# Filter cross terms moved from the matrix engine to the vector engine, with a new plan of steps, in a fused spectral filter and MLP kernel

## The chip, the cores and the metric

The kernel runs on one core of one Trainium2 chip. The metric is the device time of one execution in microseconds (us), and a number given for a kernel is the median of its runs.

Engines are named as in the profile: PE is the matrix engine (TensorE), PEld its weight loads, DVE is VectorE, ACT is ScalarE, POOL is GpSimd, SP is the engine that issues most DMA transfers (SPq is its queue). "PEclk" is the clock that was granted to PE, as a share of full speed.

## The reference

The first part filters each of eight batches along the sequence with a Fourier transform; the second is an MLP with a "snake" activation.

```python
def _attn_ref(x, filt_r, filt_i):          # x: (8, 3008, 256)
    X = np.fft.rfft(x, axis=1)
    Y = X * (filt_r + 1j * filt_i)[None]   # 1505 frequencies
    return np.fft.irfft(Y, n=3008, axis=1)

def _moe_ref(x, w_in, w_out, alpha):       # x: (24064, 256), d_ff = 2048
    h = x @ w_in
    s = np.sin(alpha * h)
    g = h + s * s / (alpha + 1e-09)
    return g @ w_out
```

## The kernel before

The transform is factored as 3008 = 47 x 64. Each batch passes three spectral stages, with a trip through DRAM (write, then load in another order) between them:

- Stage 1 (8 pieces): a transform of length 47 (`pa` matmuls). The result goes from tile `t` to DRAM buffer `d1` and comes back as tile `t2`.
- Stage 2 (13 pieces, two of 24 classes each): a transform of length 64 (`pb`), an ACT copy to `xf`, multiplication by the filter on DVE, and the inverse transform (`pc`). The result goes from tile `g` through DRAM buffer `d2` to tile `t4`.
- Stage 3 (16 pieces): the inverse of length 47 (`pd`), which fills `y`, the MLP's input.

A complex product needs four real products. The upper 64 partitions of `xf` hold imaginary parts, the lower 64 real parts. The kernel before makes two full 128-partition products on DVE, one with the real and one with the imaginary filter, and lets PE do the crossing: two inverse matmuls per class with two weight tables add up in PSUM.

```python
nc.scalar.copy(out=xf, in_=ps)
pr = []
for k in range(2):
    pt = ppool.tile([128, 2, C], FP16, ...)
    nc.vector.tensor_tensor(out=pt, in0=xf, in1=f_t[k][:, 2 * u:2 * u + 2, :], op=ALU.mult)
    pr.append(pt)
# [...]
for i in range(2):
    for k in range(2):                                   # two matmuls per class
        nc.tensor.matmul(out=ps[:, i, :], lhsT=e_t[:, k, 2 * w + i, :],
                         rhs=pr[k][:, i, :], start=(k == 0), stop=(k == 1))
```

The MLP is a loop of 384 "steps", 48 per batch. A step issues two blocks of the hidden matmul (`ph`), a cosine on ACT, one fused DVE operation that makes the snake (`v`), and about one block of the output projection (`po`, eight matmuls). Spectral pieces of later batches are put in between the steps by a plan: a piece of batch `b` is issued at step 48*b plus the number given.

```python
plan = {1: [-45 + i for i in range(8)],                  # stage 1: -45 to -38
        2: [-29 + 14 * i / 13 for i in range(13)],       # stage 2: from -29
        3: [-10, -9] + [-7 + 2 * i for i in range(14)]}  # stage 3: from -10
# [...]
fps = pool("fps", 2, PSUM)     # the two banks that all spectral matmuls share
hps = pool("hps", 4, PSUM)     # four banks for the hidden matmul
```

## Time and profile before

| | before |
|---|---|
| median (range) of the first three runs | 840.68 us (840.13 to 840.93) |
| PE, DVE, ACT busy | 96%, 75%, 73% |
| inverse matmuls `pc` | 384 |

The first fence has lines of the profile's page of the kernel before: busy time by engine, the busy tenths of PE, DVE and the granted clock in 40 slices of the span, and the shares of the chain of waits.

```profile
PE 799.8 (96%) x5793; PEld 544.2 (65%) x5793; DVE 628.1 (75%) x1119; ACT 613.0 (73%) x1200; POOL 28.3 (3%) x55
PE   5758999999999999999999999999999999999996
DVE  3658886778877788777877788777877778777772
PEclk9969999999999999999999999999999999999999
PE 83%; DMA 7%; ACT 4%; issue 3%; DVE 2%; POOL 0%; SPq 0%; ACTq 0%; DVEq 0%; POOLq 0%
```

PE is full from the fifth slice to the last but one, at full clock, and the chain that ended last is PE work. DVE has a quarter of its time free. The Trainium skill (Trainium Kernel Development and Optimization, "Performance Expectations") warns that matmul busy time is a bad metric for how close a kernel is to roofline, because matmuls are pipelined; here the view by windows helps, since a gap of PE can be seen in it, and it shows none between 150 and 800 us.

Next come two groups of the page before (columns: line, engine, operation, output<-inputs, shapes, count | busy us, mean ns of one | idle before, releaser).

```profile
L187 DVE TENSOR_TENSOR p<-xf,filt 128x512 f16<-128x512 f16 x192 | 72.1, 419 | 4.9 <-ACT xf L183 4.5
L199 PE MATMUL pc<-p,e_t 128*128 128x256 f16 x384 | 59.7, 275 | 2.6 <-DVE p L187 1.5
```

A product lasts 419 ns, but four in a row take 1.43 us, as the timeline of DVE in the kernel before shows (columns: start, length, what, count):

```profile
28.39 1.43 DVE L187 TENSOR_TENSOR p<-xf,filt 128x512 f16<-128x512 f16 x4 [4.54 <-ACT xf L183]
```

So they start (1.43 - 0.42) / 3 = 0.34 us apart: one begins before the other has ended. For `pc`, 275 ns is latency; in the steady part eight matmuls with 256 columns take 0.88 us, 0.110 us each.

### The profile page before, as it was taken

To read this page: it belongs to the slowest core of one execution; us is meant where nothing else is said; L and a number is where in the kernel's file an instruction comes from. 1 tells how busy PE (TensorE), PEld (TensorE's weight loads), DVE (VectorE), ACT (ScalarE), POOL (GpSimd) and SP (SyncE) were. 2 spreads that over 40 slices of the span, in tenths; PEclk is the share of its full clock that TensorE was granted. 3 is DMA by queue.
4 is the path that set the end of the run, shared out by engine and by line. 5 is a ranking of instruction groups with operands and counts; after the bars stand their busy time and mean duration, and the time that the engine had idled before them with its cause. 6 is when DMAs were issued, how large, how long until landed. Compare 5 with 4: busy or idle time off the path is not lost.

```text
span 837.2 us, 16122 instructions
## 1 busy us (share of the span) xinstructions
PE 799.8 (96%) x5793; PEld 544.2 (65%) x5793; DVE 628.1 (75%) x1119; ACT 613.0 (73%) x1200; POOL 28.3 (3%) x55
## 2 busy tenths in 40 slices
PE   5758999999999999999999999999999999999996
PEld 2425676667776677666776677666777677666674
DVE  3658886778877788777877788777877778777772
ACT  4536886787868787787877777777877878677763
POOL 3210000000000000000000000000000000000000
PEclk9969999999999999999999999999999999999999
DMA  9985835185344744266242763447443353421111
GB/s 220 218 255 117 200 89 130 51 174 116 82 135 81 171 99 109 75 141 153 65 130 60 165 137 82 115 91 171 92 96 94 97 113 83 115 58 38 38 40 45
DMA packets 93495, 94.98 MB, mean 113 GB/s; under 512 B 8084, under 2 KB 82852, under 8 KB 93416
## 3 DMA queue, kind: packets, MB, share of 16 engines
q1 hardware_dynamic: 84784, 75.02, 34.5%
q0 software_dynamic: 6704, 18.09, 12.5%
q10 hardware_dynamic: 1928, 0.86, 0.5%
q8 instruction: 45, 0.74, 0.3%
q14 instruction: 34, 0.28, 0.1%
HBM read 58.02 MB, written 49.81 MB: 129 GB/s over the span
## 4 chain that ended last, share of the span: by engine, by line
PE 83%; DMA 7%; ACT 4%; issue 3%; DVE 2%; POOL 0%; SPq 0%; ACTq 0%; DVEq 0%; POOLq 0%
PE po L369 36%; PE ph L354 35%; PE pc L199 4%; PE pa L157 3%; ACT cos L357 2%; PE pd L219 2%; PE pb L180 2%; DMA t<-d 1%; DMA w_out<-in_moe_w_out_dram 1%; DMA d<-g 1%; DMA d_t<-d_tbl 1%; DVE p L187 1%; DMA x<-in_x_dram 1%; DMA filt<-in_filt_i_dram 1%; ACT t L135 1%
## 5 line engine op out<-in xcount | busy, mean ns | idle before, releaser
L358 DVE SCALAR_TENSOR_TENSOR v<-cos,ph 128x512 f16<-128x512 f32 (+1 forms) x768 | 484.0, 672 | 164.0 <-ACT cos L357 163.5
L357 ACT ACTIVATE cos<-ph 128x512 f32<-128x512 f32 (+1 forms) x768 | 411.6, 589 | 153.9 <-PE ph L354 152.5
L369 PE MATMUL po<-w,v 128*128 128x256 f16 x3008 | 400.9, 273 | 2.6 <-DVE w L337 2.6
L354 PE MATMUL ph<-y,w 128*128 128x512 f16 (+1 forms) x1536 | 391.5, 377 | 0.2 <-ACT y L135 0.2
L369 PEld LDWEIGHTS <-v 128*128 128x128 f16 x3008 | 289.0, 98 | 80.9 <-issue 8.7
L354 PEld LDWEIGHTS <-w 128*128 128x128 f16 x1536 | 150.4, 98 | 101.0 <-issue 4.6
L187 DVE TENSOR_TENSOR p<-xf,filt 128x512 f16<-128x512 f16 x192 | 72.1, 419 | 4.9 <-ACT xf L183 4.5
L375 ACT COPY o<-po 128x512 f32<-128x512 f32 x96 | 55.6, 579 | 17.7 <-PE po L369 15.5
L135 ACT CAST t<-pa 96x512 f16<-96x512 f32 x89 | 51.0, 589 | 19.0 <-PE pa L157 18.9
L183 ACT CAST xf<-pb 128x512 f16<-128x512 f32 x96 | 57.0, 595 | 8.1 <-PE pb L180 5.5
L219 PEld LDWEIGHTS <-t 96*128 96x128 f16 x512 | 36.3, 100 | 39.8 <-DMA t<-d 11.8
L199 PE MATMUL pc<-p,e_t 128*128 128x256 f16 x384 | 59.7, 275 | 2.6 <-DVE p L187 1.5
L157 PE MATMUL pa<-x,wf_t 94*96 94x512 f16 x128 | 47.2, 408 | 10.1 <-DMA x<-in_x_dram 6.3
L219 PE MATMUL pd<-wi_t,t 96*128 96x94 f16 x512 | 43.4, 208 | 11.1 <-DMA t<-d 10.9
L135 ACT CAST y<-pd 128x376 f16<-128x376 f32 x82 | 39.1, 479 | 12.5 <-PE pd L219 12.5
L199 PEld LDWEIGHTS <-e_t 128*128 128x128 f16 x384 | 37.6, 99 | 15.6 <-issue 7.1
L180 PE MATMUL pb<-t,d_t 128*128 128x256 f16 x192 | 38.2, 283 | 2.5 <-DMA t<-d 1.5
L135 ACT CAST g<-pc 128x512 f16<-128x512 f32 x64 | 38.7, 605 | 1.6 <-PE pc L199 1.6
L137 DVE CAST t<-pa 96x512 f16<-96x512 f32 x39 | 26.6, 683 | 15.8 <-PE pa L157 15.8
L180 PEld LDWEIGHTS <-d_t 128*128 128x128 f16 x192 | 18.9, 101 | 23.8 <-issue 4.6
L118 POOL DMA_DIRECT2D x<-in_x_dram x32 | 16.7, 524 | 502.8 <-PE pa L157 490.5
L157 PEld LDWEIGHTS <-wf_t 94*96 94x96 f16 x128 | 16.6, 129 | 19.6 <-issue 9.9
(28 smaller groups left out, 94.3 us busy)
## 6 DMA issues: line engine op xcount, KB each, us to landing
d<-t SPq DMA_DIRECT2D x32, 384.0 KB
d<-g SPq DMA_DIRECT2D x64, 192.0 KB
t<-d SPq DMA_DIRECT2D x32, 384.0 KB
x<-in_x_dram POOLq DMA_DIRECT2D x32, 376.0 KB, 6.9
t<-d SPq DMA_DIRECT2D x60, 192.0 KB
out_dram<-o SPq DMA_DIRECT2D x72, 94.0 KB
w_in<-in_moe_w_in_dram POOLq DMA_DIRECT2D x2, 1024.0 KB, 9.2
w_out<-in_moe_w_out_dram POOLq DMA_DIRECT2D x1, 2048.0 KB, 11.6
```

The costliest lines, as they stand in the source:

```text
L135: marks["act"] = nc.scalar.copy(out=dst, in_=src)
L157: marks["pe"] = nc.tensor.matmul(out=ps[0:NK, :], lhsT=wf_t, rhs=st["x"][ch][:, n0:n0 + 2, :], start=True, stop=True)
L180: nc.tensor.matmul(out=ps[:, i, :], lhsT=d_t[:, s, :], rhs=st["t2"][s // 6][:, s % 6, :], start=True, stop=True)
L183: nc.scalar.copy(out=xf, in_=ps)
L187: marks["prod", u] = nc.vector.tensor_tensor(out=pt, in0=xf, in1=f_t[k][:, 2 * u:2 * u + 2, :], op=ALU.mult)
L199: nc.tensor.matmul(out=ps[:, i, :], lhsT=e_t[:, k, 2 * w + i, :], rhs=pr[k][:, i, :], start=(k == 0), stop=(k == 1))
L219: nc.tensor.matmul(out=psv[:, i, :], lhsT=st["t4"][:, 4 * half + i, cb * 128:cb * 128 + 128], rhs=wi_t, start=True, stop=True)
L354: nc.tensor.matmul(out=ps[:, 0:n], lhsT=w1[:, cb, jb * 128:jb * 128 + 128], rhs=y_cols[:, cb, c0:c0 + n], start=(cb == 0), stop=(cb == 1))
L357: nc.scalar.activation(out=cs[:, 0:n], in_=ps[:, 0:n], func=AFT.Sin, bias=float(np.pi / 2))
L358: marks["snake"] = nc.vector.scalar_tensor_tensor(out=v[k][:, jb, 0:n], in0=cs[:, 0:n], scalar=-1.0, in1=ps[:, 0:n], op0=ALU.add, op1=ALU. ...
L369: nc.tensor.matmul(out=pso[k][:, t % 2, :], lhsT=v[k][:, jb, 128 * t:128 * t + 128], rhs=w2[:, jb, :], start=(jb == 0), stop=(jb == 15))
L375: nc.scalar.copy(out=o[:, 0:nb, :], in_=pso[k][:, 0:nb, :])
```

## The change

From batch 2 on (`FUSED = 2`), DVE does the crossing too: two products of 64 partitions that read one half and write the other, one full product, and an addition in place. Then one inverse matmul per class is enough. This takes 6 batches x 24 classes = 144 matmuls from PE and adds two DVE instructions per piece. To make room on DVE, stage 2 is spread over 24 steps instead of 14, fewer PSUM evacuations go to DVE (one in five instead of one in three), and stage 1 and 3 are moved to fit. Stage 3's loads are issued one ahead, and the pool of the products has 6 buffers instead of 4.

```diff
-        flip[0] = (flip[0] + 1) % 3
+        flip[0] = (flip[0] + 1) % 5
@@ (stage 2, cut)
+            if 0 <= u - 1 < 12:
+                new_products(u - 1)
+                prod(nc.vector, 1, u - 1, lo, hi)      # reads partitions 0-63, writes 64-127
+                prod(nc.vector, 1, u - 1, hi, lo)
+                prod(nc.vector, 0, u - 1, every, every)
+            w = u - 1
+            if 0 <= w < 12:
+                p0, p1 = st["p", w]
+                nc.vector.tensor_tensor(out=p0, in0=p0, in1=p1, op=ALU.add)
+                st["p", w].pop()
+            if 0 <= w - 1 < 12:
+                inverse(w - 1)                          # one matmul per class
@@ (stage 3, cut)
+                for c in ([0, 1] if ch == 0 else [ch + 1] if ch < 3 else []):
+                    load_t4(c)
@@ (plan, cut)
-    plan = {1: [-45 + i for i in range(8)],
-            2: [-29 + 14 * i / 13 for i in range(13)],
-            3: [-10, -9] + [-7 + 2 * i for i in range(14)]}
+        if b == 1 and stage < 3:
+            return 8 + i if stage == 1 else 23 + i
+        odd = b % 2
+        return 48 * b - 4 * odd + (-50 + i if stage == 1 else -36 + 24 * i / 13 if stage == 2
+                                   else -6 + i if i < 4 else -1 + 2 * (i - 4))
```

(The signs of two tables change with it: the filter's second copy is negated instead of the inverse table.) In the new plan stage 1 ends at -43 and stage 2 begins at -36: 7 steps where there were 9.

More of the change, by code (lines that the diff above doesn't have):

```diff
@@ L22 @@
 NK = 4 * NS
+FUSED = 2
 def dft_tables():
@@ L92 @@
     xfpool = pool("xf", 3)
-    ppool = pool("pp", 4)
+    ppool = pool("pp", 6)
     gpool = pool("gp", 4)
@@ L171, in stage1, with forward @@
                     st["t2"].append(t2)
+        def forward(u):
+            ps = (ops if b == 0 else fps).tile([128, 2, C], FP32, name=f"pb_{b}_{u}",
+                                               tag="o" if b == 0 else "f")
+            for i in range(2):
+                s = 2 * u + i
+                nc.tensor.matmul(out=ps[:, i, :], lhsT=d_t[:, s, :],
+                                 rhs=st["t2"][s // 6][:, s % 6, :], start=True, stop=True)
+            xf = xfpool.tile([128, 2, C], FP16, name=f"xf_{b}_{u}", tag="xf")
+            nc.scalar.copy(out=xf, in_=ps)
+            st["xf", u] = xf
@@ new lines, in inverse @@
+        def inverse(w):
+            pr = st.pop(("p", w))
+            if w % 3 == 0:
+                st["g"] = gpool.tile([128, 6, C], FP16, name=f"g_{b}_{w}", tag="g")
+            ps = fps.tile([128, 2, C], FP32, name=f"pc_{b}_{w}", tag="f")
+            for i in range(2):
+                for k, pt in enumerate(pr):
+                    nc.tensor.matmul(out=ps[:, i, :], lhsT=e_t[:, k, 2 * w + i, :],
+                                     rhs=pt[:, i, :], start=(k == 0), stop=(k == len(pr) - 1))
+            i0 = 2 * (w % 3)
+            evac(st["g"][:, i0:i0 + 2, :], ps, i0 != 2 if b == 0 else None)
+            if w % 3 == 2:
+                for p in range(2):
+                    a0 = p * NS + 6 * (w // 3)
+                    nc.sync.dma_start(out=d2[a0:a0 + 6, :, :].rearrange("s n c -> n s c"),
+                                      in_=st["g"][64 * p:64 * p + 64, :, :])
@@ new lines, in prod, with new_products, stage2_first @@
+        def prod(eng, k, u, rows, to):
+            marks["prod", u] = eng.tensor_tensor(out=st["p", u][k][to, :, :], in0=st["xf", u][rows, :, :],
+                                                 in1=f_t[k][rows, 2 * u:2 * u + 2, :], op=ALU.mult)
+        def new_products(u):
+            st["p", u] = [ppool.tile([128, 2, C], FP16, name=f"p_{b}_{u}_{k}", tag="p") for k in range(2)]
+        lo, hi, every = slice(0, 64), slice(64, 128), slice(0, 128)
+        def stage2_first(u):
+            if u < 12:
+                forward(u)
+                new_products(u)
+                for k in range(2):
+                    prod(nc.vector, k, u, every, every)
+            if u > 0:
+                inverse(u - 1)
@@ L173, in stage2 @@
         def stage2(u):
             if u < 12:
-                ps = (ops if b == 0 else fps).tile([128, 2, C], FP32, name=f"pb_{b}_{u}",
-                                                   tag="o" if b == 0 else "f")
-                for i in range(2):
-                    s = 2 * u + i
-                    nc.tensor.matmul(out=ps[:, i, :], lhsT=d_t[:, s, :],
-                                     rhs=st["t2"][s // 6][:, s % 6, :], start=True, stop=True)
-                xf = xfpool.tile([128, 2, C], FP16, name=f"xf_{b}_{u}", tag="xf")
@@ L183, in stage2 @@
-                nc.scalar.copy(out=xf, in_=ps)
-                pr = []
-                for k in range(2):
-                    pt = ppool.tile([128, 2, C], FP16, name=f"p_{b}_{u}_{k}", tag="p")
-                    marks["prod", u] = nc.vector.tensor_tensor(out=pt, in0=xf, in1=f_t[k][:, 2 * u:2 * u + 2, :],
-                                                               op=ALU.mult)
-                    pr.append(pt)
-                st["p", u] = pr
-            if u > 0:
-                w = u - 1
-                pr = st.pop(("p", w))
-                if w % 3 == 0:
-                    st["g"] = gpool.tile([128, 6, C], FP16, name=f"g_{b}_{w}", tag="g")
-                ps = fps.tile([128, 2, C], FP32, name=f"pc_{b}_{w}", tag="f")
-                for i in range(2):
-                    for k in range(2):
-                        nc.tensor.matmul(out=ps[:, i, :], lhsT=e_t[:, k, 2 * w + i, :],
-                                         rhs=pr[k][:, i, :], start=(k == 0), stop=(k == 1))
-                i0 = 2 * (w % 3)
-                evac(st["g"][:, i0:i0 + 2, :], ps, i0 != 2 if b == 0 else None)
-                if w % 3 == 2:
-                    for p in range(2):
-                        a0 = p * NS + 6 * (w // 3)
-                        nc.sync.dma_start(out=d2[a0:a0 + 6, :, :].rearrange("s n c -> n s c"),
-                                          in_=st["g"][64 * p:64 * p + 64, :, :])
@@ new lines, in stage2 @@
+                forward(u)
+            if 0 <= u - 1 < 12:
[10 more added lines that the diff above has]
+                inverse(w - 1)
@@ L209, in stage3, with load_t4 @@
+        def load_t4(ch):
+            st["t4", ch] = t4pool.tile([NK, 8, C], FP16, name=f"t4_{b}_{ch}", tag="t4")
+            marks["t4"] = nc.sync.dma_start(out=st["t4", ch], in_=d2_rows[:, 8 * ch:8 * ch + 8, :])
         def stage3(u):
@@ L212, in stage3 @@
             if rest == 0:
-                t4 = t4pool.tile([NK, 8, C], FP16, name=f"t4_{b}_{ch}", tag="t4")
-                marks["t4"] = nc.sync.dma_start(out=t4, in_=d2_rows[:, 8 * ch:8 * ch + 8, :])
-                st["t4"] = t4
+                for c in ([0, 1] if ch == 0 else [ch + 1] if ch < 3 else []):
+                    load_t4(c)
             ps = fps.tile([128, 4, 128], FP32, name=f"pd_{b}_{u}", tag="f")
@@ L219, in stage3 @@
                 nc.tensor.matmul(out=psv[:, i, :],
-                                 lhsT=st["t4"][:, 4 * half + i, cb * 128:cb * 128 + 128],
+                                 lhsT=st["t4", ch][:, 4 * half + i, cb * 128:cb * 128 + 128],
                                  rhs=wi_t, start=True, stop=True)
@@ L226, in spectral @@
             pieces.append((1, lambda u=u: stage1(u)))
-        for u in range(13):
-            pieces.append((2, lambda u=u: stage2(u)))
+        for u in range(13 if b < FUSED else 14):
+            pieces.append((2, lambda u=u: (stage2_first if b < FUSED else stage2)(u)))
         for u in range(16):
@@ L266, in dup_filter @@
         gs = slice(6 * g, 6 * g + 6)
-        for k in range(2):
-            ins = nc.vector.tensor_copy(out=f_t[k][64:128, gs, :], in_=f_t[k][0:64, gs, :])
+        for ins in (nc.vector.tensor_copy(out=f_t[0][64:128, gs, :], in_=f_t[0][0:64, gs, :]),
+                    nc.vector.tensor_scalar(out=f_t[1][64:128, gs, :], in0=f_t[1][0:64, gs, :],
+                                            scalar1=-1.0, scalar2=None, op0=ALU.mult)):
             behind(ins, marks["prod", 3 * g - 2] if g else s1_dve)
@@ L288 @@
         nc.vector.tensor_copy(out=e_t[0:64, 1, gs, :], in_=e_t[64:128, 0, gs, :])
-        nc.vector.tensor_scalar(out=e_t[64:128, 1, gs, :], in0=e_t[0:64, 0, gs, :],
-                                scalar1=-1.0, scalar2=None, op0=ALU.mult)
+        nc.vector.tensor_copy(out=e_t[64:128, 1, gs, :], in_=e_t[0:64, 0, gs, :])
     ones = cpool.tile([128, 128], FP32)
@@ L391, in store, with at_step @@
             p += cnt
-    plan = {1: [-45 + i for i in range(8)],
-            2: [-29 + 14 * i / 13 for i in range(13)],
-            3: [-10, -9] + [-7 + 2 * i for i in range(14)]}
+    def at_step(b, stage, i):
+        if b == 1 and stage < 3:
[3 more added lines that the diff above has]
+                                   else -6 + i if i < 4 else -1 + 2 * (i - 4))
     pending = [(1 + i % 4 + 8 * (i // 4), 0, piece) for i, (_, piece) in enumerate(first[25:])]
@@ L402 @@
         for stage, piece in spectral(b):
-            at_step = 48 * b + plan[stage][at[stage]]
-            if b == 1 and stage < 3:
-                at_step = 8 + at[stage] if stage == 1 else 23 + at[stage]
+            pending.append((at_step(b, stage, at[stage]), b, piece))
             at[stage] += 1
-            pending.append((at_step, b, piece))
     pending.sort(key=lambda p: p[0])
```

## The prediction

> **What bounds the kernel now.** TensorE. The page gives PE 96% busy, DVE 75%, ACT 73%; in the view by windows every 50 us stretch from 150 to 800 us has PE busy for 49.8 to 50.0 us at clock 1.00. The chain of waits is 83% PE. DVE's longest wait is for ACT's cosine (163 us in all), ACT's for the hidden matmul (152 us): followers, not limits. Before the steady part lie about 54 us of start-up, after it about 14 us of tail.
>
> **Removed from PE.** Six batches x 24 classes lose one of two inverse matmuls: 144 matmuls with 256 columns. The page's mean of 275 ns is latency; in the timeline eight such matmuls take 0.88 us, so each is worth 0.110 us. 144 x 0.110 = 15.8 us, all on the bottleneck.
>
> **Added to DVE.** Per piece, four tensor_tensor of 512 elements replace two; half the partitions makes none shorter. In a row the old products start 0.34 us apart although one lasts 0.42 us. The Trainium skill (VectorE: DVE Perf Modes, "Two Vector instructions with no wait between them") says that an instruction whose inputs or output start in another quadrant than the previous one's starts only when all earlier ones are finished. That hits the two crossed products and the one after them. The trace agrees: the crossed filter copies of the start-up do not overlap (two take 1.14 us, mean 0.56). So a piece costs about 0.34 + 3 x 0.42 = 1.6 us instead of 0.68: +66 us over 72 pieces. The evacuation count of 5 instead of 3 moves 43 casts from DVE to ACT (order of instructions): about -24 us DVE, +21 us ACT. DVE rises to roughly 665 us busy, ACT to 635.
>
> **Where it meets the critical path.** I cut the instruction order into MLP steps and summed durations. Before, a stage-2 step has 2.40 us of PE and about 2.1 us of DVE. After, spread over 24 steps, PE has 1.95 to 2.15 us per step and DVE 2.0 to 2.45: DVE becomes the local limit for about half of each batch period, by 0.1 to 0.3 us a step. Four hidden PSUM banks and the piece-long lag of the inverse absorb some 2 us; the rest stalls PE. Estimate: 0.5 to 2 us per batch, 3 to 10 us in all, centre 5.
>
> **Start-up.** The first two loads of stage 3 are now issued together and the w_out load waits for the second; the first projection already waited for w_out. +1 to 2 us. Stage 3 still ends long before its columns are read; it should cost nothing.
>
> **Sum.** 840.7 - 15.8 + 1.5 + 5 = 831.5 us, about 1.1% faster. Range 824.5 to 839. Faster by over 2% (below 823.9) needs no DVE stall and a start-up gain: 0.13. Within 2%: 0.84. Slower by over 2%: 0.03.
>
> **What would show each step.** Inverse matmuls 384 -> 240, PE busy about 15 us less. Four products per piece, the 64-partition ones as long (0.42 us) as the full ones; DVE busy 655 to 690 us. In the windows, stage-2 stretches show DVE above 95% and PE losing 0.5 to 2 us per batch, waiting for DVE (snake freeing hidden banks, or the add before the inverse), while other stretches stay full. First projection 1 to 2 us later.
>
> **What would make it wrong.** Crossed products dearer than 0.45 us: at 0.5 us each the backlog would lose 15 to 25 us, no gain left. Fewer stalls than I assume, or a shorter start-up: down to 822. DVE lag holding an evacuation that PE needs at once makes the slack smaller than 2 us.

## More of the kernel before

Between the last piece of stage 1 and the first of stage 2 lie 9 steps.

Last, the trip through DRAM between stages 1 and 2, for batch 3 (batches count from 0), as the timeline of the kernel before has it:

```profile
275.40 0.60 PE L157 MATMUL pa<-x,wf_t 94*96 94x512 f16 x2
277.24 0.32 SPq L161 DMA_DIRECT2D d<-t  x1
286.03 5.69 SPq L169 DMA_DIRECT2D t<-d  x8
292.32 0.38 PE L180 MATMUL pb<-t,d_t 128*128 128x256 f16 x2
```

The last stage-1 matmul, the issue of the last write, the issue of the loads (SP holds them back until the write has landed), and the first stage-2 matmul are 16.9 us from end to end. PE does not wait for any of it: the line of the first `pb` names no idle time. So 16.9 us is the room that the plan leaves, not what the trip takes. As an estimate, the trip takes about 15.3 us: 10.6 us to the issue of the load, and 4.65 us from issue to data, as in batch 0, where PE waits for them (loads issued at 22.50 us, first `pb` at 27.15 us).

## The result

The changed kernel takes 863.85 us (median of 4 runs, 860.46 to 867.72), the kernel before 840.8 us in the same rounds. The ratio is 1.0271 (95% interval 1.0222 to 1.032): slower by 2.7%. A ratio here is the mean time of one kernel's runs over that of the other's of the same rounds, so it is not quite the ratio of the medians quoted. The result is correct.

The same lines of the page, of the changed kernel:

```profile
PE 799.6 (92%) x5649; PEld 532.8 (62%) x5649; DVE 663.4 (77%) x1218; ACT 635.1 (73%) x1245; POOL 28.2 (3%) x55
PE   6747998999999899998999899998999999999996
DVE  2656785769977699767996699766997799877772
PEclk9978999999999899999999899999999999999998
PE 48%; DVE 26%; DMA 14%; ACT 7%; issue 3%; SPq 1%; ACTq 0%; DVEq 0%; POOLq 0%
```

PE has 144 matmuls fewer and yet the same busy time, 799.6 against 799.8 us. The clock row tells part of why: in two slices deep in the steady part, and in two of the start-up instead of one, the granted clock is below 0.9, and a matmul at half clock is busy about twice as long (eight take 1.91 instead of 1.04 us in the example below). DVE and DMA now hold 40% of the chain of waits. DVE's busy rows have full stretches (99) and emptier ones between them, one pair per batch.

The groups that answer to those shown before; the product group has two forms now, of 64 and of 128 partitions:

```profile
L204 DVE TENSOR_TENSOR p<-xf,filt 64x512 f16<-64x512 f16 (+1 forms) x264 | 108.7, 420 | 22.3 <-ACT xf L183 18.0
L234 DVE TENSOR_TENSOR p<-p,p 128x512 f16<-128x512 f16 x72 | 30.2, 419 | 0.4
L193 PE MATMUL pc<-p,e_t 128*128 128x256 f16 x240 | 44.4, 282 | 9.2 <-DVE p L234 3.2
```

A product of 64 partitions lasts as long as a full one, and `pc` has dropped from 384 to 240, as predicted. DVE's busy time too is as predicted (663.4 against about 665 us).

What was not predicted stands in the list of who waited for whom, of PE from 148 us to the end (columns: total us, times, longest us). The kernel before has no such line in that stretch.

```profile
PE pb L180 <- DMA t<-d: 14.6, 5, 4.2
PE pc L193 <- DVE p L234: 3.2, 3, 1.7
PE pc L193 <- DVE y L138: 2.7, 4, 1.3
PE ph L387 <- DVE v L391: 1.4, 6, 0.4
PE pc L193 <- DVE g L138: 1.1, 1, 1.1
```

Five batches (2 to 6) wait 2.0 to 4.2 us each for the load in front of stage 2. Here is batch 3 in the timeline of the changed kernel:

```profile
268.28 0.69 PE L158 MATMUL pa<-x,wf_t 94*96 94x512 f16 x2
269.26 0.51 POOL L119 DMA_DIRECT2D x<-in_x_dram  x1 [3.82 <-PE pa L158]
269.79 0.32 SPq L162 DMA_DIRECT2D d<-t  x1
279.88 5.28 SPq L170 DMA_DIRECT2D t<-d  x8
284.06 0.58 PE L180 MATMUL pb<-t,d_t 128*128 128x256 f16 x2 [4.17 <-DMA t<-d]
284.44 1.91 PE L402 MATMUL po<-w,v 128*128 128x256 f16 x8
```

(The POOL line is the last of four loads of the next batch's input; it will matter in e11.) The load is issued 9.8 us after the write was (279.88 - 269.79 - 0.32), and its data come 4.2 us later. PE reaches the stage-2 matmul at 279.89 and stands still for 4.17 us. And then eight projection matmuls take 1.91 us instead of the 1.04 us that the timeline gives them elsewhere. The view by windows shows the reason (columns: window, its length, then for each engine busy us and count, then granted clock, DMA share, GB/s):

```profile
275.00:280.00 5.00, 4.89 (x36) 2.99 (x33) 4.13 (x7) 4.05 (x10) 0.00 (x0) 1.00 0.17 51
280.00:285.00 5.00, 0.94 (x5) 0.71 (x6) 1.28 (x2) 0.90 (x3) 0.00 (x0) 0.81 0.73 173
285.00:290.00 5.00, 5.00 (x24) 2.95 (x23) 2.98 (x6) 1.82 (x4) 0.00 (x0) 0.50 0.96 183
```

After the gap, PE runs at half clock for five microseconds and looks fully busy with 24 matmuls instead of about 36. The Trainium skill (TensorE: Matmul & The Clock Gate, "Why this matters for your kernels") says to leave no PE-idle gap over about 3 us between bursts, or the clock falls to half. The trace agrees for the gap of 4.17 us; it also shows a fall (0.66 on average from 395 to 400 us) after a gap of only 2.22 us, and none after one of 2.44 us at 599 us.

The loss of this kind adds up: 14.6 us of waits, plus half-clock stretches worth about 5.0 x (0.50 + 0.48 + 0.34) = 6.6 us (windows at 285, 490 and 395 us with clocks 0.50, 0.52, 0.66), together about 21 us.

### The profile page after: what moved, and what is told of

The parts are those of the page before. It is cut to its first block, busy times and chain, and to the rows that moved or that the text cites. A ratio compares the mean times of both kernels' runs of the same rounds, so it can differ in the third digit from the quotient of the medians.

```text
span 865.8 us, 15865 instructions
## 1 busy us (share of the span) xinstructions
PE 799.6 (92%) x5649; PEld 532.8 (62%) x5649; DVE 663.4 (77%) x1218; ACT 635.1 (73%) x1245; POOL 28.2 (3%) x55
## 4 chain that ended last, share of the span: by engine, by line
PE 48%; DVE 26%; DMA 14%; ACT 7%; issue 3%; SPq 1%; ACTq 0%; DVEq 0%; POOLq 0%
PE po L402 21%; PE ph L387 20%; DVE v L391 14%; DVE p L204 8%; DMA d<-t 6%; DMA t<-d 5%; ACT cos L390 4%; PE pa L158 3%; DVE p L234 2%; ACT t L136 2%; DMA w_out<-in_moe_w_out_dram 2%; PE pc L193 1%; PE pd L252 1%; ACT y L136 1%; PE pb L180 1%
## 5 line engine op out<-in xcount | busy, mean ns | idle before, releaser
L387 PE MATMUL ph<-y,w 128*128 128x512 f16 (+1 forms) x1536 | 397.1, 378 | 2.4 <-DVE v L391 1.8
L204 DVE TENSOR_TENSOR p<-xf,filt 64x512 f16<-64x512 f16 (+1 forms) x264 | 108.7, 420 | 22.3 <-ACT xf L183 18.0
L136 ACT CAST t<-pa 96x512 f16<-96x512 f32 x99 | 57.0, 595 | 18.2 <-PE pa L158 17.9
L136 ACT CAST y<-pd 128x376 f16<-128x376 f32 x105 | 50.3, 481 | 13.5 <-PE pd L252 13.5
L158 PE MATMUL pa<-x,wf_t 94*96 94x512 f16 x128 | 49.0, 413 | 10.4 <-DMA x<-in_x_dram 6.3
L252 PE MATMUL pd<-wi_t,t 96*128 96x94 f16 x512 | 44.0, 210 | 12.8 <-DMA t<-d 11.6
L193 PE MATMUL pc<-p,e_t 128*128 128x256 f16 x240 | 44.4, 282 | 9.2 <-DVE p L234 3.2
L136 ACT CAST g<-pc 128x512 f16<-128x512 f32 x76 | 46.2, 608 | 6.2 <-PE pc L193 6.1
L193 PEld LDWEIGHTS <-e_t 128*128 128x128 f16 x240 | 23.4, 100 | 20.1 <-issue 7.5
L138 DVE CAST t<-pa 96x512 f16<-96x512 f32 x29 | 19.8, 683 | 18.9 <-PE pa L158 18.9
L234 DVE TENSOR_TENSOR p<-p,p 128x512 f16<-128x512 f16 x72 | 30.2, 419 | 0.4
```

What stands on the lines that cost most here:

```text
L136: marks["act"] = nc.scalar.copy(out=dst, in_=src)
L158: marks["pe"] = nc.tensor.matmul(out=ps[0:NK, :], lhsT=wf_t, rhs=st["x"][ch][:, n0:n0 + 2, :], start=True, stop=True)
L204: marks["prod", u] = eng.tensor_tensor(out=st["p", u][k][to, :, :], in0=st["xf", u][rows, :, :], in1=f_t[k][rows, 2 * u:2 * u + 2, :], op= ...
L252: nc.tensor.matmul(out=psv[:, i, :], lhsT=st["t4", ch][:, 4 * half + i, cb * 128:cb * 128 + 128], rhs=wi_t, start=True, stop=True)
L387: nc.tensor.matmul(out=ps[:, 0:n], lhsT=w1[:, cb, jb * 128:jb * 128 + 128], rhs=y_cols[:, cb, c0:c0 + n], start=(cb == 0), stop=(cb == 1))
```

## The experiments

Twelve kernels were run. Two theories stood against each other at first:

- Round trip: the new plan leaves 7 steps (11.6 us for batch 3, from 268.28 to 279.89 us) for a trip through DRAM that took 15.8 us there. (The expectations below put it at 14 us, which is too much.)
- VectorE: the added DVE products hold PE up.

As a measure that leaves the start-up out, this table also gives the time from the first stage-2 matmul of batch 4 to that of batch 6 in the timeline: two batch periods in the steady part, with the same work in each kernel but for the inverse matmuls (48 fewer with the new arithmetic; at 0.110 us that is 5.3 us, so 194.5 - 5.3 = 189.2 us would be the whole gain).

| kernel | median us | ratio to before | two batch periods us |
|---|---|---|---|
| before | 839.6 to 840.8 (four sets of rounds) | | 194.5 |
| changed | 863.85 | 1.0271 | 206.2 |
| e1_gap9 | 842.49 | 1.0029 | 195.4 |
| e2_two_matmuls | 864.94 | 1.0285 | 204.3 |
| e3_before_gap7 | 854.17 | 1.0153 | 200.7 |
| e4_wout_first | 861.15 | 1.0253 | 205.8 |
| e6_gap9_two_matmuls | 841.49 | 1.0025 | 194.2 |
| e7_spread30 | 842.49 | 1.0029 | 193.9 |
| e7b_spread30_b1 | 838.98 | 0.9973 | 199.3 |
| e8_gap9_uncrossed (wrong result) | 827.46 | 0.9849 | 189.5 |
| e9_pairs | 837.31 | 0.9965 | 190.7 |
| e10_pairs_start | 832.04 | 0.9916 | 190.6 |
| e11_x_after | 843.10 | 1.0040 | 196.1 |
| e12_all | 830.88 | 0.9897 | 190.3 |

### e1_gap9: only stage 1 two steps earlier

```diff
-        return 48 * b - 4 * odd + (-50 + i if stage == 1 else ...
+        return 48 * b - 4 * odd + (-52 + i if stage == 1 else ...
```

> Changed kernel with only stage 1 started two MLP steps earlier, so that 9 steps instead of 7 lie between the last stage-1 matmul of a batch and its first stage-2 matmul, as in the kernel before. Round-trip theory (the intermediate's write to DRAM and load back takes 15 to 16 us, the new plan leaves 14): the five waits of 2.0 to 4.2 us of the first stage-2 matmul for its load vanish, and with them the stretches at half clock behind them; 863.9 falls to 838 to 848 us. Rival theory (the added VectorE products are the cost): the load waits may go, but PE then stands behind VectorE, and the time stays above 855 us.

Measured: 842.49 us, 21.4 us less than the changed kernel, about the 21 us summed above. PE's waits after 148 us in this run (four largest lines):

```profile
PE pc L193 <- DVE y L138: 3.8, 4, 1.3
PE pc L193 <- DVE p L234: 3.1, 3, 1.7
PE ph L387 <- DVE v L391: 1.4, 6, 0.4
PE pc L193 <- DVE g L138: 1.3, 1, 1.3
```

The wait of `pb` for its load is gone, and so is every window of reduced clock from 150 us to the tail. The round trip was the cause of the slowdown (e2, e3 and e11 test this from other sides). But the kernel still is not faster than before, although PE has 15.8 us less to do. What is left are waits of PE for DVE.

### e2_two_matmuls: the new plan with the old arithmetic

```diff
-FUSED = 2
+FUSED = 8
```

> Changed kernel with the old arithmetic in all batches (two products, two inverse matmuls per class), but the new plan of steps. Round-trip theory: waits for the stage-2 load of about 2 to 4 us in most batches and half-clock stretches stay, PE has 15.8 us more work: 855 to 875 us. Rival theory (VectorE): it falls back to 838 to 846 us.

Measured: 864.94 us, with 14.1 us of `pb` waiting for its load in five batches. The slowdown stays without any of the new DVE work, so the plan alone makes it; the new arithmetic is worth about nothing (863.85 against 864.94 us).

### e3_before_gap7: the kernel before with the shorter distance

```diff
-    plan = {1: [-45 + i for i in range(8)],
+    plan = {1: [-43 + i for i in range(8)],
```

> Kernel before with only stage 1 moved two steps later (7 instead of 9 steps before stage 2). Before, last stage-1 matmul to load issue took 8 to 11 us and load to data about 4.2 us, so 12 to 15 us are needed where 13 to 14.5 are left. Round-trip theory: waits of 0.5 to 2.5 us for the stage-2 load appear in some batches, 843 to 855 us. Rival theory: no change, at most 842 us.

Measured: 854.17 us, slower by 1.5% (ratio 1.012 to 1.0186: clear of 1), with 10.4 us of `pb` waiting for its load in five batches, the longest 4.0 us. Two steps of distance taken from the old kernel make it slow in the same way.

### e4_wout_first: start-up

The load of the output weights waits for the first stage-3 load again, instead of for the second.

```diff
-            marks["t4"] = nc.sync.dma_start(out=st["t4", ch], ...)
+            ins = nc.sync.dma_start(out=st["t4", ch], ...)
+            marks["t4"] = ins
+            if ch == 0:
+                marks["t4_first"] = ins
@@ (load of w_out)
-          marks["t4"])
+          marks["t4_first"])
```

> Changed kernel with the w_out load behind the first stage-3 load instead of the second. Start-up theory: the first projection starts at about 65 instead of 68.7 us and the whole time falls by 3 to 6 us, to 858 to 861 us; the stage-2 waits stay. If the late first projection is due to something else, nothing moves.

Measured: the first projection starts at 65.0 us instead of 68.7 (64.8 in the kernel before), and the whole takes 861.15 us, 2.7 us less where 3 to 6 were expected; the intervals of the two ratios to before overlap, so the totals do not settle this. The start times do so only together, since each is that of one profile and they scatter: 66.9 to 68.7 us in the six profiles with the changed start-up (changed kernel, e1, e2, e6, e8, e11), 65.0 to 66.2 with the load order mended (e4, e7, e7b), 64.8 and 65.9 with the old start-up (before, e3). The runs with wider products start later for a reason told there.

### e6_gap9_two_matmuls: what the arithmetic is worth once the load is in time

This is e1_gap9 with `FUSED = 8`.

> e1_gap9 (9 steps between stage 1 and 2) with the old arithmetic in all batches: the time less that of e1_gap9 (842.5 us) is what the one-matmul arithmetic is worth once the load waits are gone. If PE alone counted, 15.8 us: 858 us. With the VectorE waits that e1_gap9 shows (about 8.5 us in eight gaps of PE, plus short ones), 847 to 852 us. If the new arithmetic is worth nothing here, 842 to 844 us.

Measured: 841.49 us against 842.49 us for e1_gap9. With the loads in time, the new arithmetic still gains nothing: the third of the expected outcomes. All of the 15.8 us saved on PE is given back; that it goes into waits for DVE is shown by the next run.

### e8_gap9_uncrossed: the same number of products, none crossing partitions

Its output is wrong, which doesn't matter for the time. Two full, uncrossed products take the place of the two crossed ones, so that as many instructions of the same length run.

```diff
-                prod(nc.vector, 1, u - 1, lo, hi)
-                prod(nc.vector, 1, u - 1, hi, lo)
+                prod(nc.vector, 1, u - 1, every, every)
+                prod(nc.vector, 1, u - 1, every, every)
```

> Wrong result on purpose: e1_gap9 with the two crossed 64-partition products made full, uncrossed ones, so that as many products of the same length run, but none changes quadrant. Hold theory: products again start 0.34 instead of 0.42 to 0.45 us apart, VectorE's busy time falls by 10 to 20 us and PE's waits for VectorE shrink: 834 to 840 us. If crossing costs nothing, busy time and total stay (661 and 842 us).

Measured: 827.46 us, 15.0 us less than e1_gap9, and less than expected. The same stretch of stage 2 in the view by windows, first of e1_gap9, then of e8_gap9_uncrossed:

```profile
195.00:245.00 50.00, 49.09 (x346) 33.38 (x345) 48.35 (x95) 40.07 (x78) 0.00 (x0) 1.00 0.29 71
```

```profile
195.00:245.00 50.00, 50.00 (x360) 34.92 (x359) 46.91 (x97) 41.66 (x82) 0.00 (x0) 1.00 0.30 74
```

With crossing, DVE is busy 97% and PE does 346 matmuls in 50 us; without, it does 360 at a DVE load of 94%. PE's busy time hardly shows the difference (49.1 against 50.0 us with 14 matmuls fewer), so most of the waiting is counted as busy in this view. DVE's total busy time falls by 16.5 us (661.2 to 644.7), although there are as many instructions and each lasts as long (420 and 418 ns). It is the overlap that crossing takes away. The timeline of DVE in the changed kernel shows it:

```profile
230.08 0.42 DVE L234 TENSOR_TENSOR p<-p,p 128x512 f16<-128x512 f16 x1
230.53 0.85 DVE L204 TENSOR_TENSOR p<-xf,filt 64x512 f16<-64x512 f16 x2
231.41 1.29 DVE L391 SCALAR_TENSOR_TENSOR v<-cos,ph 128x512 f16<-128x512 f32 x2
232.62 0.42 DVE L204 TENSOR_TENSOR p<-xf,filt 128x512 f16<-128x512 f16 x1
232.95 1.28 DVE L391 SCALAR_TENSOR_TENSOR v<-cos,ph 128x512 f16<-128x512 f32 x2
```

The full product at 232.62 is followed by the snake at 232.95, 0.33 us later, before the 0.42 us are over. The addition at 230.08 is followed by the crossed product at 230.53, 0.45 us later, and the instruction behind the two crossed products starts at 231.41, 0.88 us for two. This agrees with what the Trainium skill (VectorE: DVE Perf Modes, "Two Vector instructions with no wait between them") says of instructions that start in another quadrant than the one before. As an estimate, the cost is about 0.08 us each (0.42 - 0.34), some three times a piece: 16.5 us / 72 pieces = 0.23 us.

The kernel before shows the same in its start-up: a crossed filter copy starts at 29.85 us, just after a product has ended at 29.82, while a second copy that crosses the same way starts 0.48 us after the first, although one lasts 0.55 us. This fits a cost of changing direction rather than of crossing as such, but it is one pair of copies.

With 189.5 us for two batch periods this run reaches almost the whole gain (189.2 us). So 0.23 us per piece on an engine with a fifth of its time free (DVE is busy 79% in e1) decided whether the change pays.

### e7_spread30 and e7b_spread30_b1: stage 2 over 30 steps

```diff
-  -50 + i if stage == 1 else -36 + 24 * i / 13 if stage == 2
+  -58 + i if stage == 1 else -42 + 30 * i / 13 if stage == 2
```

The load order of e4 is included. e7b also has stages 1 and 2 of batch 1 two steps earlier (`6 + i` and `21 + i`).

> Changed kernel with stage 2 over 30 instead of 24 MLP steps, stage 1 eight steps earlier (9 steps between), and w_out behind the first stage-3 load. Per step VectorE then has about 2.0 us against 1.95 to 2.1 of PE, so that PE's waits for VectorE (8.5 us in e1_gap9) should mostly go, and the start-up loses 1.5 to 2.5 us: 829 to 835 us, below the kernel before. If those PE waits are not from VectorE's load per step but from the order of instructions, it stays at 838 to 842 us.

> e7_spread30 with stages 1 and 2 of batch 1 two steps earlier, so that stage 2 ends 5 instead of 3 steps before stage 3: the wait of 2.5 us for the stage-3 load at 141 to 144 us, and the half clock behind it, should go, 2 to 4 us less than e7_spread30. If the earlier stage 1 then waits for its x load, nothing is won.

Measured: 842.49 us, not the 829 to 835 expected. PE's waits for DVE after 148 us did fall, to 2.3 us for `y` and shorter ones, but a new wait came: `pd` for its stage-3 load, 2.9 and 2.8 us in batches 2 and 4. In this plan stage 1 of the next batch runs at the same time as that load; whether its transfers delay the load, and which, was not taken apart. e7b took 838.98 us (834.43 to 840.69). The wait at 141 to 144 us went, as expected, but its profiled run has one of these stage-3 waits of 5.4 us, which is why its two batch periods are long. Moving one stage brought another trip through DRAM into trouble.

### e9_pairs and e10_pairs_start: wider products

The crossed arithmetic stays, but the products of two pieces are made together, with 1024 elements a partition. The inverse comes two pieces later, and three pools are cut to make room (`xf` 3 to 2, `pp` 6 to 4, `gp` 4 to 3 buffers). The distance of 9 steps is that of e1.

```diff
+            m, odd = divmod(u - 2, 2)
+            if 0 <= m < 6:
+                xx, fs = st["xx", m], slice(4 * m, 4 * m + 4)       # four classes at once
+                if not odd:
+                    for src, to in ((lo, hi), (hi, lo)):
+                        nc.vector.tensor_tensor(out=st["pp", m][1][to, :, :], in0=xx[src, :, :],
+                                                in1=f_t[1][src, fs, :], op=ALU.mult)
+                else:
+                    nc.vector.tensor_tensor(out=p0, in0=xx, in1=f_t[0][:, fs, :], op=ALU.mult)
+                    nc.vector.tensor_tensor(out=p0, in0=p0, in1=p1, op=ALU.add)
@@ (plan)
-  -50 + i if stage == 1 else -36 + 24 * i / 13 if stage == 2
+  -52 + i if stage == 1 else -36 + 24 * i / 15 if stage == 2
```

> e1_gap9 with the VectorE products of two pieces taken together: the same crossed arithmetic, but four instructions with 1024 elements a partition per two pieces instead of eight with 512 (three buffers fewer or smaller to make room; the inverse comes two pieces later). If a product is about 0.15 us fixed and 0.27 us per 512 elements,[...] one with 1024 lasts 0.68 to 0.70 us, VectorE's busy time falls from 661 to 630 to 645 us, and PE's waits for VectorE shrink as in e8_gap9_uncrossed: 826 to 834 us, correct. If quadrant changes as such, not VectorE's time, hold PE, it stays at 838 to 843 us.

> e9_pairs with the two start-up mends (w_out behind the first stage-3 load; stages 1 and 2 of batch 1 two steps earlier). 3 to 6 us less than e9_pairs if the start-up theory holds: 821 to 830 us; the same as e9_pairs if it does not.

Measured for e9_pairs: 837.31 us, above the expected range, but correct and below the kernel before. The groups of DVE in this run:

```profile
L239 DVE TENSOR_TENSOR pp<-xx,filt 64x1024 f16<-64x1024 f16 x72 | 49.4, 686 | 1.8
L244 DVE TENSOR_TENSOR pp<-pp,pp 128x1024 f16<-128x1024 f16 x36 | 24.8, 688 | 0.3
L243 DVE TENSOR_TENSOR pp<-xx,filt 128x1024 f16<-128x1024 f16 x36 | 24.7, 686 | 0.1
```

A product with 1024 elements lasts 0.686 us where two with 512 that do not overlap last 0.84, and DVE's busy time is 644.7 us, the same as in e8_gap9_uncrossed. (0.42 and 0.686 us give, as an estimate, 0.15 us fixed and 0.27 us per 512 elements.) The steady part is as expected: 190.7 us for two batch periods. This fits that crossing itself does not hold PE, but the time that it costs DVE does. It is not shown by this run alone, because the edit also gives the inverse two more pieces of time, and that was not tested by itself.

The total missed its range. The profiled run is 10.2 us longer than that of e8_gap9_uncrossed. Of this, 3.2 us lie before the first projection (71.1 against 67.9 us): batch 0's inverse waits 3.3 us for an evacuation into `g`, a wait that only the runs with three `g` buffers instead of four have. The other 7 us come later and are not taken apart; one wait of 1.3 us for a stage-2 load, in batch 3, is among them, so even 9 steps have little to spare. e10_pairs_start, with both start-up mends, takes 832.04 us, 5 us less: the difference is as expected, while the range of 821 to 830 us was missed.

### e11_x_after: is the write slow by itself?

The changed kernel with its 7 steps; only the input load of the next batch is held back until this batch's stage-2 load has landed.

```diff
+            if b > 1:
+                after(ins, marks["t2", 3])
```

> Changed kernel with its 7 steps between stage 1 and 2, but the input load of the next batch waits until this batch's stage-2 load has landed, instead of starting as soon as stage 1 frees its buffers. Contention theory (the write takes 9 us because the next input load shares the DMA engines with it): the wait of the load for the write falls from 9 to 4 to 6 us, the PE gaps of 2 to 4 us vanish without moving the plan, and the time comes down to 840 to 848 us. If the write is slow by itself, the gaps and 860 to 866 us stay.

Measured: 843.10 us, 20.8 us less than the changed kernel, with no step of the plan moved. Batch 3 in this run's timeline:

```profile
264.51 0.32 SPq L164 DMA_DIRECT2D d<-t  x1
267.51 5.28 SPq L172 DMA_DIRECT2D t<-d  x8
274.44 0.38 PE L182 MATMUL pb<-t,d_t 128*128 128x256 f16 x2
278.06 2.04 POOL L119 DMA_DIRECT2D x<-in_x_dram  x4 [86.45 <-PE ph L389]
```

The load follows the write after 2.7 us instead of 9.8, and the data are there before PE wants them. The write was slow because the next batch's input load, which starts as soon as stage 1 frees its buffers, was on the DMA engines at the same time: in the changed kernel the last part of that load is issued at 269.26 us and the write at 269.79 us. In the kernel before it is slow too (8.5 us for batch 3), but 9 steps hide it. Batch 7, which has no next input, agrees in both: 2.7 us. The Trainium skill (DMA: Bandwidth & Descriptors, "Queues, rings and completion order") says that each DMA engine takes turns between the queues that have work, packet by packet; that fits a write that waits behind another queue's loads, but no run here shows the single packets.

### e12_all: everything together

This is e10_pairs_start with the input load held back.

> e10_pairs_start with the input load held back as in e11_x_after. With 9 steps between stage 1 and 2 the load waits are gone already, so no more than 2 us either way against e10_pairs_start, unless the held-back load comes too late for the next stage 1.

Measured: 830.88 us, ratio 0.9897 (0.9882 to 0.9912): correct, and 1.0% faster than the kernel before. Against e10_pairs_start (832.04) it is within what was expected. It still has the wait for a `g` buffer in the start-up (3.8 us), so it is not the end of the road.

## Why the prediction was wrong, point by point

- Taken off PE, 15.8 us: right. e8_gap9_uncrossed against e6_gap9_two_matmuls, with and without the 144 matmuls at the same distance, gives 14.0 us; the two batch periods give 4.7 of 5.3 us.
- DVE's and ACT's busy time (about 665 and 635 us predicted, 663.4 and 635.1 measured), the length of the 64-partition products and the loss of overlap at a change of quadrant: right.
- "Stage 3 still ends long before its columns are read; it should cost nothing": no wait for it shows after 148 us. In batch 1 the first `pd` waits 2.5 us for its load (1.6 us in the kernel before), and the mean clock from 145 to 150 us is 0.66, against 1.00 in the kernel before. More important, it was the only distance in the plan that I checked. The distance from stage 1 to stage 2, cut from 9 to 7 steps, has no term in the sum. This is the step that failed. It cost 21.4 us (e1), in waits and in the half clock behind them; e2, e3 and e11 show it from three other sides. The round trip could be estimated from the profile before: about 15.3 us in the example, of which the write held the load for 8.5, inside a distance of 16.9 us. That left less than 2 us to spare, and the plan took away two steps (7 steps were 11.6 us for batch 3).
- "3 to 10 us in all, centre 5" for PE's stalls behind DVE: the mechanism was right, the size was not. What crossing adds alone costs 15.0 us (e1 against e8). The estimate let the hidden banks and the lag of the inverse absorb 2 us. The waits show the weaker place: the largest line is `pc` waiting for DVE to evacuate one of the two spectral banks (3.8 us of `y`, 1.3 us of `g`), up to 1.3 us at a time, behind DVE's backlog. The prediction named this danger last and gave it no number.
- Start-up, +1 to 2 us: somewhat low. The first projection came 3.9 us later in the pair of profiles shown, 1 to 4 us over all profiles (see e4). With the order of loads mended it starts at 65.0 to 66.2 us again, so that order explains it; in the total it is worth about 2.7 us, within the scatter.
- "PE losing 0.5 to 2 us per batch, while other stretches stay full": the other stretches did not stay full; that is where the load waits are. "PE busy about 15 us less" failed too: it stayed at 799.6 us, since half clock and short waits count as busy.

The terms as measured: -15.8 + 21.4 + 15.0 + 2.7 = +23.3 us, beside the +23.1 us between the medians. The experiments overlap a little and the 2.7 us lie within the scatter, so this close an agreement is partly luck.

## What to carry to other kernels

When a plan moves stages that talk through DRAM, check every write-to-load distance against the round trip measured in the trace, with the transfers that will run beside it, and not only the last one before the consumer. A PE wait of a few microseconds can cost half as much again in clock (here 14.6 us of waits and 6.6 us of clock), and then part of the loss hides in PE's busy time, so compare a stretch of fixed work, such as two batch periods, rather than busy shares. When work moves to an engine with average slack, what counts is its load in the stretch where the work lands: there, 0.08 us per crossing instruction took the whole gain, and the kernel with instructions twice as wide got most of it back in the steady part (190.7 us for two batch periods, against 195.4 with crossing and 189.5 without).

## What the Trainium skill lacked or had wrong

- TensorE: Matmul & The Clock Gate: its advice is about gaps over about 3 us. Here a PE gap of 2.22 us was followed by reduced clock (0.66 over the five microseconds from 395 us), and one of 2.44 us was not.
- DMA: Bandwidth & Descriptors: I found no figure there for how much a write to DRAM is stretched by loads beside it. Here the load could follow the last 384 KB write of stage 1 after 2.7 us when the next input load was held back (e11), and after 8.6 to 9.8 us beside it (changed kernel, batches 2 to 6).
- VectorE: DVE Perf Modes: the rule on quadrants agreed with the trace, but that section gives no cost. Here it was about 0.08 us per held instruction (an estimate), 16.5 us of DVE time in 72 pieces.
